# Split attention and a max-out MLP on one core: first loads in another order, score runs cut alike, the whole order planned anew

## The chip, the cores and the metric

The kernel runs on one core of a Trainium2 chip. The metric is the device time of one execution in microseconds, as the median of several runs. PE is the matmul engine (PEld its weight loads), DVE, ACT and POOL (GpSimd) are the vector, scalar and general engines, SP (SyncE) issues most DMAs. SBUF is the on-chip memory, PSUM holds matmul results in eight banks.

## What is computed

Attention over 4 batches, 8 heads, 768 positions, head size 64. Three "retrieval" heads see all earlier positions; the five others see 4 sink positions and a window of 64. Its output, as 3072 rows of 512, goes through an MLP that takes the larger of two products.

```python
scores = scale * np.matmul(q, k.transpose(0, 1, 3, 2))
mask = np.where(retr, causal, causal & (is_sink | in_win))   # by head
a = softmax(np.where(mask, scores, -1e9))
x = np.matmul(a, v)          # transposed to [B * S, H * D] = [3072, 512]
g = np.maximum(x @ w1, x @ w2)
out = g @ w_out
```

The kernel uses max(h1, h2) = relu(h1 - h2) + h2: with w12 = w1 - w2 and w2o = w2 @ w_out it computes out = relu(x @ w12) @ w_out + x @ w2o.

## The kernel before

**Tiling.** Each batch is cut in two halves of 384 query positions, (b, hf). Heads go in pairs; `SLOTS` says which pairs hold full (F) and which windowed (S) heads. In the text A = (0,0), B = (0,1), C = (1,0).

**Stages of a half.** q, k (768 KB each) and v (three pieces of 256 KB) are loaded into one of three slots of `ld`. They are cast to bf16 (`cast_qk`, `cast_v` into `vb`), q and k are turned by PE (L756) and copied from PSUM (`unturn`, into `qk`); for windowed heads the sink blocks are joined to window blocks (`mix_k`, `mix_v`, tiles `kx`, `vx`). Scores are matmuls in groups of two PSUM banks (L945; for A a bias at L919), exponentials run on ACT (L964), masks on DVE (L983), attention times v is L1008, normalising L1025 and L1035. The result x is turned, by PE for batch 0 (L1128) and by DMA for the others, into `xt`. Then come eight up blocks of 4 matmuls (L1219), a relu each (L1243 or L1245, on ACT or DVE), and three output blocks of 12 down matmuls (L1269), copied out by ACT or DVE (`ot`) and stored by SP (L1288).

**Weights.** w1 and w2 are loaded as f32 in halves of 1 MB (L637): w2 into the third slot of `ld`, w1 into the slot of A, so that w1 has to wait until A's q, k and v have been cast. w_out goes in four loads through GpSimd's queue, which cast to bf16 (L651). `prep_weights` casts w2, turns it (L1180), multiplies it with w_out in 32 matmuls (L1198) and subtracts w1 - w2 in four quarters on DVE (L1164). The first up block needs the first of these quarters.

**The order.** Nothing is scheduled by hand. Every piece of work is an `Op` with costs per engine, dependencies and a rank. `Order.run` plays them through a model of the engines, the DMA queues and the PSUM banks, and emits each instruction when the model starts it. So constants such as `RANK`, `FRONT`, `MARGIN`, `RATE`, `DMA_LATE` and `RING` (how much may be outstanding on a queue) decide the order of each engine's instructions, and nothing else. The engines then run these orders with real waits. Where the model leaves PE idle in the first 38 us, it puts in matmuls on a tile `warmer` (L503). `LOADS` names the order in which the first loads are asked for: A and B are q and k of a half, Av and Bv its v, wo0 to wo3, w10 to w21 the weights.

A load of w_out waits for an earlier load by way of a one-element copy on GpSimd (`landed`, L650); `PACE` says how far behind in the flow.

Of the kernel before, what the change touches and what calls it, by code (L numbers as in the profile page):

```python
# [114 lines left out]
class Op:  # L115
# [4 lines left out]
        "claims", "frees", "margin", "tag", "port", "bias", "share", "parts", "grain",  # L120
    )

    def __init__(self, costs, emit, deps=(), lat=0.13, data=None, rank=0.0, claims=(), frees=(),
                 margin=0.0, tag=None, port=(), bias=None, share=1.0, parts=1024, grain=18.0):
        self.costs, self.emit, self.lat, self.data, self.rank = costs, emit, lat, data, rank
        self.deps = [o for o in deps if o is not None]
        self.claims, self.frees, self.margin, self.tag = claims, frees, margin, tag
        self.port, self.bias, self.share, self.parts = port, bias or {}, share, parts
        self.grain = grain
        self.end, self.ready, self.users = None, 0.0, []  # L130


class Order:
# [6 lines left out]
    def __init__(self, banks, dummy, dummies_until):  # L140
        self.ops, self.lists, self.n, self.shift, self.stuck = [], {}, 0, 0.0, False
        self.banks, self.freed = [None] * banks, [0.0] * banks
        self.at, self.dummy, self.dummies_until = {}, dummy, dummies_until
# [36 lines left out]
    def release(self, key, t):  # L180
        key, part = key if isinstance(key[-1], list) else (key, None)
        for e in self.at[key] if part is None else [self.at[key][part[0]]]:
            assert self.banks[e] == key
            self.banks[e], self.freed[e] = None, t
# [12 lines left out]
    def run(self, names, allowed):  # L197
        free = dict.fromkeys(("PE", "ACT", "DVE", "POOL", "SP"), 0.0)
        free["SP"], free["PE"] = 0.75, PE_BEGINS
# [26 lines left out]
        def begin(o, e, t, extra=0.0):  # L226
            cost = o.costs[e] + extra
            if e in o.port:
                wait = max(0.0, port[0] - t)
                cost += wait  # L230
                port[0] = t + cost
            free[e] = t + cost
            if e == "PE":
                done_pe.append((t, t + cost, o.share))
            o.emit(e)
            trace.append((t, e, cost, o))
            push(t + cost, None)
            if o.data is None:
                push(t + cost + o.lat, o)
            else:  # L240
                asked[e] += o.parts
                push(t + (DMA_FIRST if t < 1.0 else DMA_LATE[e]), (e, o))

# [34 lines left out]
        for t in (0.0, free["SP"], free["PE"]):  # L278
            push(t, None)
# [107 lines left out]
    'cast': 8.0, 'vcast': 10.45, 'unturn': 6.55, 'mix_k': -4.7, 'mix_v': -16.7, 'exp': 3.7,  # L387
    'mask': -7.6, 'norm': -7.5, 'take_x': -1.15, 'turn': 0.05, 'w2b': 5.75, 'sub': -6.2, 'w2t':
    -4.8, 'wob': -3.6, 'w2o': -3.6, 'relu': 3.45, 'load': 6.6, 'out': -5.4, 'h2': 7.9, 'table':
    -3.65, 'vload': -0.55,  # L390
# [14 lines left out]
LOADS = ('A', 'wo0', 'B', 'w20', 'w10', 'Av', 'wo1', 'wo2', 'w11', 'wo3', 'w21', 'Bv')  # L405
# [11 lines left out]
DMA_LATE = {'SP': 2.7, 'POOL': 3.2, 'ACT': 2.2}  # L417
RING = {'SP': 4224, 'POOL': 6200, 'ACT': 4224}
SPLIT = ((0, 0), (0, 1))
K_BY_ACT = False  # L420
# [7 lines left out]
    'first': 0.26, 'long': 0.32, 'v': 0.235, 'w': 0.355, 'w half': 0.39, 'wo': 0.37, 'cast':  # L428
    0.22,
}  # L430
SPARE = {}
STEP = 3.5
FF_STEP = -2.8
# [9 lines left out]
MARGIN = {'W': 1.2, 'S': 0.3, 'F': 0.3, 'TQ': 1.2}  # L443
X_MARGIN = 0.8
FRONT = (
    {'mix_k': -14.4, 'mask': -3.2, 'unturn': 13.5, 'exp': 11.7, 'vcast': 31.8, 'cast': -27.9,
    'norm': -5.0}, {'vcast': 9.0, 'unturn': -0.2, 'exp': 16.7, 'mask': 0.7, 'norm': -5.5,
    'mix_k': 13.8, 'cast': -1.4},
)
FRONT_STEP = (22.5, 5.2)  # L450
UNTURN_BIAS = ({'ACT': 1.0}, {})
SHARED = 0.89
UP_PARTS = 2


def tile_three_full_heads(
# [36 lines left out]
    landed = keep.tile([1, 1], F32, name="landed")  # L493
# [13 lines left out]
    eng = {"ACT": nc.scalar, "DVE": nc.vector, "POOL": nc.gpsimd}  # L507
    T = {}
# [18 lines left out]
    def dma(mb, emit, deps=(), rate=0.31, rank=0.0, old=None, parts=1024, grain=18.0):  # L527
        asked.append(rank)
        o = op({"SP": 0.5}, emit, deps, data=mb / rate, rank=rank + 1e-4 * len(asked), parts=parts, grain=grain)
        if old is not None:  # L530
            later.append((o, old))
        return o
# [4 lines left out]
    def slot():  # L537

        s = PLACES[number[0]]
        number[0] += 1  # L540
        old, freed[s] = freed.get(s, []), []
        return s, old, freed[s]

    def load_half(b, hf, kinds=(0, 1, 2)):
# [4 lines left out]
        def whole(t, src):  # L549
            def emit(_):  # L550
                nc.sync.dma_start(  # L551
                    out=lds[:, s, t],
                    in_=src[b, :, rows, :].rearrange("h (p n) d -> p h (n d)", p=128),
                )
            mb = 1.572 if early_k and (b, hf) == (0, 0) else 0.786
            loads[b, hf, t].append(dma(mb, emit, old=old, rate=RATE["first"] if t == 0 and (b, hf) != (0, 0) else RATE["long"], grain=36.0))

        def piece(t, src, i):
            def emit(_):
                r0 = HALF * hf + 128 * i  # L560
                nc.sync.dma_start(
                    out=lds[:, s, t, :, i * D:i * D + D],
                    in_=src[b, :, r0:r0 + 128, :].rearrange("h p d -> p h d"),
                )
            loads[b, hf, t].append(dma(0.262, emit, old=old, rate=RATE["v"]))
# [26 lines left out]
    def load_pair(b, p):  # L592
# [32 lines left out]
        tenants[b].append(un)  # L625
        return un, [got[2, 0], got[2, 1]]

    def load_up(name, src, c):

        if name not in T:  # L630
            s, staged_old[name], tenants[name] = slot()
            T[name] = lds[:, s].rearrange("p t h c -> p (t h c)")[:, 0:KC * d_ff] \
                .rearrange("p (c f) -> p c f", f=d_ff)
        n = d_ff // UP_PARTS

        def emit(_):
            nc.sync.dma_start(  # L637
                out=T[name][:, :, c * n:c * n + n],
                in_=src.rearrange("(c p) f -> p c f", p=128)[:, :, c * n:c * n + n],
            )  # L640
        return dma(
            2.097 / UP_PARTS, emit, old=staged_old[name], rate=RATE["w"] if UP_PARTS == 4 else RATE["w half"],
            parts=512, grain=180.0 / UP_PARTS,
        )

    def load_down(c, behind):

        def emit(_):
            for o in behind:
                nc.gpsimd.tensor_copy(out=landed, in_=place_of[o])  # L650
            nc.gpsimd.dma_start(  # L651
                out=wob[:, 2 * c:2 * c + 2],
                in_=wo.rearrange("(c p) f -> p c f", p=128)[:, 2 * c:2 * c + 2],
            )
# [7 lines left out]
    for what in LOADS:  # L662
        kind, c = what[:2], int(what[2:]) if what[:1] == "w" else 0
        if what[0] in "ABCD":
# [4 lines left out]
            for n, o in enumerate(loads[(*of, kinds[-1])]):  # L669
                last = (n if kinds[-1] == 2 or of not in LONG else NT - 1) * D  # L670
                place_of[o] = lds[0:1, slot_of[of], kinds[-1], 0, last:last + 1]
        elif kind == "wo":
            wo_in[c] = load_down(c, flow[-1 - PACE:len(flow) - PACE])
        else:
# [3 lines left out]
            place_of[got[c]] = T[kind + "f"][0:1, 0, c * d_ff // UP_PARTS:c * d_ff // UP_PARTS + 1]  # L678
# [47 lines left out]
    def cast_qk(n, hf, hh, lo=0, hi=2):  # L726
        b, p = first_half(n)

        def emit(e):
            src = lds[:, slot_of[b, hf], lo:hi, bass.ds(heads[2 * p + hh], 1), :]  # L730
# [30 lines left out]
    def unturn(n, hf, lo=0, hi=2):  # L761
        def emit(e):
            src = bank(("pt", n, hf, lo), BF16)[:, 0:(hi - lo) * HALF].rearrange("f (t c) -> f t c", t=hi - lo)
# [61 lines left out]
    def prepare(b, hf, p):  # L825
# [7 lines left out]
        else:  # L833
# [4 lines left out]
            for hh in range(2):  # L838
                for lo, hi in ((0, 1), (1, 2)) if (b, hf) in SPLIT else ((0, 2),):
                    cs.append(op(  # L840
# [4 lines left out]
                    ))  # L845
            casts[n, hf] = cs
# [11 lines left out]
            tenants[b, hf] += cs + (vs if b not in V_BY_DMA else [])  # L858
# [8 lines left out]
            else:  # L867
                last_turn[n, hf], turned[n, hf] = [], []
                for lo, hi in ((0, 1), (1, 2)) if (b, hf) in SPLIT else ((0, 2),):
                    key, m = ("pt", n, hf, lo), hi - lo  # L870
                    tq = pe(
                        "TK" if lo else "TQ", mm(*[128] * (m * NT)), turn(n, hf, lo, hi),
                        cs[lo::2] if m == 1 else cs, claims=[(key, 1)],
# [5 lines left out]
                        frees=[key], tag=f"unturn{b}.{hf}.{p}", rank=rank_of("unturn", b, hf, p),  # L879
# [27 lines left out]
    def scores(b, hf, t):  # L907
        banks_, _, _ = group_of(b, hf)[t]

        def emit(_):  # L910
# [10 lines left out]
            for bk, blocks in enumerate(banks_):  # L921
# [9 lines left out]
                runs.append(mine)  # L931
            for step in range(max(len(r) for r in runs)):
# [113 lines left out]
    def attend(b, hf):  # L1046
        group = group_of(b, hf)
        exps, done = {}, {}
        for t in range(len(group)):
# [20 lines left out]
            for bk in range(2):  # L1070
# [4 lines left out]
                if len(at_users) > NAT:  # L1075
                    later.append((e, at_users[-1 - NAT]))
# [80 lines left out]
    def prep_weights():  # L1157
# [31 lines left out]
        tenants["w2f"] += w2b_ops + sub_ops  # L1189
        tenants["w1f"] += sub_ops  # L1190
# [164 lines left out]
    for e, old in later:  # L1355
        e.deps.extend(old)
# [323 lines left out]
```

## Time and profile before

| | us |
|---|---|
| median of 3 runs | 182.96 (182.65 to 184.0) |
| profiled run, device time | 182.93 |
| its span in the profile | 181.3 |
| PE busy | 174.2 (96%) |
| ACT busy | 132.1 (73%) |
| DVE busy | 101.7 (56%) |
| mean granted PE clock | 0.988 of full |

The span runs from the first to the last instruction of the profile; 1.63 us of the device time lie around it. In the profile a row of a group gives line, engine, operation, tiles, shapes and count, then busy us and the mean ns of one, then the idle time before them and what ended it. `ps` are the PSUM banks.

### The profile page before, as it was taken

The page shows a single profiled execution, that of the slowest core. Times are in us where ns is not written, and L with a number is a line of the kernel's source. Part 1 is how long each engine was busy: PE and PEld are TensorE (multiplying, and loading weights), DVE is VectorE, ACT ScalarE, POOL GpSimd, SP SyncE. Part 2 cuts the span into 40 slices and gives each one's busy share as a digit, 9 for nine tenths or more (in the row PEclk, how much of TensorE's full clock was granted, in tenths as well). Part 3 has the DMA queues.
Part 4 walks back from the last instruction along what each step waited for, and adds up shares of the span by engine and source line. Part 5 has one row for each costly group of instructions (what it writes and reads, how often), then busy time and mean ns, then how long its engine had stood idle before and what let it go on. Part 6 is the DMA issues. An engine that isn't in the chain of part 4 may idle for free.

```text
span 181.3 us, 4989 instructions
## 1 busy us (share of the span) xinstructions
PE 174.2 (96%) x1838; PEld 108.7 (60%) x1838; DVE 101.7 (56%) x303; ACT 132.1 (73%) x294; POOL 40.1 (22%) x80
## 2 busy tenths in 40 slices
PE   7996999999999999999989999999999999999992
PEld 7965776457657656556645775465565545545561
DVE  5685687699979998377875687247455300000000
ACT  3466846999799999999999998379694614624521
POOL 6503500200413583778930000000000000000000
PEclk9997899999999999999999999999999999999998
DMA  4999999999999999999999999620312412012013
GB/s 119 334 291 338 227 263 256 384 241 276 255 303 317 299 252 193 281 189 214 133 150 150 157 250 115 170 91 0 90 58 96 110 58 108 17 61 116 0 58 125
DMA packets 72529, 32.37 MB, mean 179 GB/s; under 512 B 53938, under 2 KB 67506, under 8 KB 72498
## 3 DMA queue, kind: packets, MB, share of 16 engines
q1 hardware_dynamic: 52448, 28.45, 62.4%
q0 software_dynamic: 19904, 3.41, 25.7%
q8 instruction: 16, 0.26, 0.6%
q14 instruction: 15, 0.12, 0.2%
q10 hardware_dynamic: 146, 0.13, 0.2%
HBM read 25.17 MB, written 6.29 MB: 174 GB/s over the span
## 4 chain that ended last, share of the span: by engine, by line
PE 70%; DMA 13%; DVE 7%; ACT 4%; issue 2%; SPq 2%; DVEq 0%; POOL 0%; ACTq 0%; POOLq 0%
PE ps L1269 31%; PE ps L1219 20%; DMA ld<-in_k_dram 7%; PE ps L945 7%; PE ps L1008 6%; DMA ld<-in_moe_w_dram 6%; PE ps L756 2%; ACT at L964 2%; DVE x L1035 2%; SPq L551 2%; PE ps L503 1%; ACT vb L512 1%; DVE at L983 1%; DVE qb L514 1%; PE ps L1198 1%
## 5 line engine op out<-in xcount | busy, mean ns | idle before, releaser
L964 ACT ACTIVATE at<-ps 128x512 bf16<-128x512 f32 (+2 forms) x134 | 66.1, 590 | 5.2 <-PE ps L945 4.5
L1269 PE MATMUL ps<-wob,g 128*128 128x512 bf16 (+1 forms) x200 | 47.6, 371 | 0.0
L1219 PE MATMUL ps<-xt,w 128*128 128x384 bf16 x256 | 45.8, 326 | 0.3 <-DVE w L1164 0.3
L983 DVE TENSOR_TENSOR at<-at,tab 128x1024 bf16<-128x1024 bf16 (+5 forms) x49 | 24.5, 514 | 14.9 <-ACT at L964 14.5
L1219 PEld LDWEIGHTS <-w 128*128 128x128 bf16 x256 | 23.5, 98 | 15.5 <-DVE w L1164 0.4
L1243 ACT ACTIVATE g<-ps 128x384 bf16<-128x384 f32 x56 | 27.8, 507 | 4.4 <-PE ps L1219 4.2
L512 ACT COPY ot<-ps 128x512 f32<-128x512 f32 (+1 forms) x21 | 12.0, 573 | 25.9 <-PE ps L1269 25.9
L1269 PEld LDWEIGHTS <-g 128*128 128x128 bf16 x200 | 18.2, 98 | 17.9 <-issue 0.2
L1269 PE MATMUL ps<-w2o,xt 128*128 128x512 bf16 (+1 forms) x100 | 24.8, 370 | 0.3 <-ACT ot L512 0.2
L1008 PEld LDWEIGHTS <-at 128*128 128x128 bf16 x477 | 20.0, 97 | 7.6 <-issue 0.2
L1035 DVE TENSOR_TENSOR x<-ps,rez 128x192 f32 x64 | 22.8, 356 | 1.8
L1008 PE MATMUL ps<-vb,at 128*128 128x65 bf16 x387 | 21.4, 193 | 0.0
L945 PE MATMUL ps<-qk 64*128 64x128 bf16 (+1 forms) x322 | 19.8, 230 | 0.1
L945 PEld LDWEIGHTS <-qk 64*128 64x128 bf16 x322 | 12.0, 94 | 9.1 <-issue 6.8
L503 PE MATMUL ps<-warmer 128*128 128x128 bf16 x149 | 14.3, 258 | 1.4 <-POOL warmer L1613 1.2
L1269 PEld LDWEIGHTS <-xt 128*128 128x128 bf16 x100 | 9.2, 98 | 9.0 <-issue 0.5
L756 PE MATMUL ps<-tab,qb 128*128 128x128 bf16 x144 | 12.6, 227 | 1.7 <-POOL qb L514 1.2
L514 POOL CAST vb<-ld 128x192 bf16 x21 | 8.1, 424 | 26.2 <-DMA ld<-in_v_dram 26.2
L503 PEld LDWEIGHTS <-warmer 128*128 128x128 bf16 x149 | 12.2, 119 | 1.5 <-POOL warmer L1613 1.2
L514 DVE COPY qk<-ps 128x384 bf16<-128x384 bf16 (+1 forms) x17 | 10.2, 642 | 3.9 <-PE ps L756 3.9
L512 ACT CAST qb<-ld 128x192 bf16 (+1 forms) x26 | 9.5, 425 | 3.8 <-DMA ld<-in_k_dram 2.0
L756 PEld LDWEIGHTS <-qb 128*128 128x128 bf16 x144 | 9.6, 101 | 3.8 <-POOL qb L514 1.4
(70 smaller groups left out, 159.6 us busy)
## 6 DMA issues: line engine op xcount, KB each, us to landing
out_dram<-ot SPq DMA_DIRECT2D x23, 256.0 KB, 2.1
ld<-in_q_dram SPq DMA_DIRECT2D x6, 768.0 KB, 7.5
ld<-in_k_dram SPq DMA_DIRECT2D x6, 768.0 KB, 7.9
ld<-in_v_dram SPq DMA_DIRECT2D x18, 256.0 KB, 6.9
ld<-in_moe_w_dram SPq DMA_DIRECT2D x4, 1024.0 KB, 11.7
wob<-in_moe_w_out_dram POOLq DMA_DIRECT2D x4, 256.0 KB, 7.8
ld<-in_q_dram POOLq DMA_DIRECT2D x8, 96.0 KB, 9.0
ld<-in_k_dram POOLq DMA_DIRECT2D x8, 96.0 KB, 9.7
```

The costliest lines, as they stand in the source:

```text
L503: nc.tensor.matmul(banks[e][:, 0:128], lhsT=warm, rhs=warm, start=True, stop=True)
L512: nc.scalar.copy(out=out, in_=in_)
L514: eng[e].tensor_copy(out=out, in_=in_)
L756: nc.tensor.transpose(to[:, i], qbs[:, T["qb", n, hf] % NQB, t, i].rearrange("p h d -> p (h d)"), ident)
L945: nc.tensor.matmul(to.rearrange("p (i c) -> p i c", c=128), lhsT=lhsT, rhs=q_of(n, i, m)[rows], start=bk not in under, stop=True, skip_gro ...
L964: nc.scalar.activation(out=at[:, bk, 0:w], in_=bank(("ps", b, hf, t), part=bk)[:, 0:w], func=ACT.Exp, scale=scale,)
L983: eng[e].tensor_tensor(out=at, in0=at, in1=tbl, op=ALU.mult)
L1008: nc.tensor.matmul(po[:, hh, i - NT * hf, :], lhsT=ats[:, T["at", b, hf, t] % NAT, bk, e * 128:(e + 1) * 128], rhs=rhs, start=first, stop= ...
L1035: nc.vector.tensor_tensor(out=xs[:, (2 * b + hf) % NX, :, bass.ds(heads[2 * p + hh], 1), :], in0=po[:, hh, :, 0:D].unsqueeze(2), in1=z[:, ...
L1219: nc.tensor.matmul(bank(key)[:, 0:HALF], lhsT=w[:, kc, fc * 128:(fc + 1) * 128], rhs=xts[:, (2 * b + hf) % NXT, :, kc, :], start=(kc == 0) ...
L1243: nc.scalar.activation(out=g, in_=ph, func=ACT.Relu)
L1269: nc.tensor.matmul(bank(key)[:, cols], lhsT=lhsT, rhs=(w2o if kind == "x" else wob)[:, c, cols], start=(e == 0), stop=(e == len(steps) - 1),)
```

## The change

Three things are changed, and much is added that stays switched off.

The first loads are asked for in another order, with w_out behind A's v:

```diff
-LOADS = ('A', 'wo0', 'B', 'w20', 'w10', 'Av', 'wo1', 'wo2', 'w11', 'wo3', 'w21', 'Bv')
+LOADS = ('A', 'B', 'Av', 'wo0', 'wo1', 'w20', 'wo2', 'wo3', 'w10', 'w21', 'w11', 'Bv')
```

Where the two banks of a group of scores hold runs of unequal number (adjacent blocks of one key block are merged into one wide matmul), all runs are cut into blocks of 128 columns:

```diff
+            if len(runs[0]) != len(runs[1]):
+                runs = [
+                    [[bk, e + j, (*blk[:-1], blk[-1] + j), 1, hh, p] for bk, e, blk, m, hh, p in mine for j in range(m)]
+                    for mine in runs
+                ]
```

The model has new limits and the constants of the order are new (ranks, steps and fronts not shown; all of them are changed):

```diff
-        free["SP"], free["PE"] = 0.75, PE_BEGINS
+        free["SP"], free["PE"], free["POOL"] = 0.75, PE_BEGINS, MASKS_MADE - 0.45
...
-                push(t + (DMA_FIRST if t < 1.0 else DMA_LATE[e]), (e, o))
+                o.late = DMA_FIRST if t < 1.0 else max(RING_LATE, DMA_LATE[e] - max(0.0, t - max(o.ready, idle[e])))
+                push(t + o.late, (e, o))
...
-DMA_LATE = {'SP': 2.7, 'POOL': 3.2, 'ACT': 2.2}
-RING = {'SP': 4224, 'POOL': 6200, 'ACT': 4224}
+DMA_LATE = {'SP': 2.7, 'POOL': 4.7, 'ACT': 2.2}
+RING_LATE = 1.0
+RING = {'SP': 3300, 'POOL': 6200, 'ACT': 4224}
...
-            parts=512, grain=180.0 / UP_PARTS,
+            parts=1536 // UP_PARTS, grain=180.0 / UP_PARTS, rank=-9.0 if by_act else 0.0,
...
-MARGIN = {'W': 1.2, 'S': 0.3, 'F': 0.3, 'TQ': 1.2}
-X_MARGIN = 0.8
+MARGIN = {'W': 0.5, 'S': 2.0, 'F': 2.0, 'TQ': 2.0}
+X_MARGIN = 0.4
```

`MARGIN` is how long an operation must have been ready, in the model, before PE takes it while other work is there; S are scores, W attention times v, F the MLP, TQ the turning of q and k.

What a slot of `ld` waits for is now kept by kind: q, k and v of a half each wait for the readers of that kind alone in the model; a weight still waits for all three.

```diff
-            loads[b, hf, t].append(dma(0.262, emit, old=old, rate=RATE["v"]))
+            loads[b, hf, t].append(dma(
+                0.262, emit, old=old[t:t + 1], rate=RATE["v"], rank=0.0 if by == "SP" else RANK["vload"], by=by,
+            ))
```

`SIX`, `BY_ACT` and `V_QUEUES`, which would lay halves out in 64 rows or send loads over other queues, are added empty, and `landed` has 128 rows in place of one for their sake.

More of the change, by code (lines that the diff above doesn't have):

```diff
@@ L845, in prepare @@
                     ))
+                    leaves((b, hf), range(lo, hi), [cast])
             casts[n, hf] = cs
@@ L857, in prepare @@
                 ))
-            tenants[b, hf] += cs + (vs if b not in V_BY_DMA else [])
+            leaves((b, hf), (2,), vs if b not in V_BY_DMA else ())
             key = ("pt", n, hf)
```

142 lines of the change are left out of this document (99 added, 43 removed).

## The prediction

> **What bounds the kernel now.** I read the page first, then the engines by stretches, then the chain of waits in order of time, then the issues of SyncE and GpSimd with the transfer rate under them. From the page (busy us, share of the span, instructions; then one group with busy us and mean ns):
>
> ```profile
> span 181.3 us, 4989 instructions
> PE 174.2 (96%) x1838; PEld 108.7 (60%) x1838; DVE 101.7 (56%) x303; ACT 132.1 (73%) x294; POOL 40.1 (22%) x80
> L503 PE MATMUL ps<-warmer 128*128 128x128 bf16 x149 | 14.3, 258 | 1.4 <-POOL warmer L1613 1.2
> ```
>
> PE is 96% busy, but 14.3 us of that is fill-in matmuls on `warmer` that compute nothing. The next rows say where PE is full of real work; columns are the stretch, its length, then busy us of PE, PEld, DVE, ACT and POOL, the granted clock, DMA share and GB/s.
>
> ```profile
> 38.10:140.00 101.90, 101.25 (x1186) 62.43 (x1187) 72.94 (x208) 90.84 (x204) 29.32 (x47) 1.00 1.11 183
> 140.00:178.00 38.00, 37.97 (x210) 20.23 (x208) 2.55 (x11) 16.35 (x32) 0.00 (x0) 1.00 0.21 75
> ```
>
> From 38.10 to 178 PE is idle 0.68 us in all, at full clock. So time can be won only before 38.10. The chain of waits (start, us, what) tells what holds that point:
>
> ```profile
> 3.84 11.87 DMA ld<-in_k_dram
> ...
> 22.87 1.31 PE ps L1198 x6
> ...
> 25.36 11.44 DMA ld<-in_moe_w_dram
> ...
> 36.82 1.24 DVE w L1164
> 38.10 2.77 PE ps L1219 x16
> 40.87 0.78 PE ps L945 x24
> 41.65 2.71 PE ps L1219 x16
> 44.36 0.88 PE ps L1008 x29
> ...
> 170.17 7.81 PE ps L1269 x48
> 178.01 0.37 ACT ot L512
> ```
>
> The first half of w1 lands at 25.36 + 11.44 = 36.80; the subtraction w1 - w2 takes 1.24; at 38.10 the first up-projection starts; 139.91 us later the last down-projection ends, at 178.01. That is the sum of the kernel: *landing of w1, plus 1.30, plus 139.9, plus the tail*. The issues of SyncE, in order, with how long each took to issue:
>
> ```profile
> 6.08 2.33 SPq L637 DMA_DIRECT2D ld<-in_moe_w_dram  x1
> 8.46 9.66 SPq L561 DMA_DIRECT2D ld<-in_v_dram  x3
> 18.16 0.93 SPq L637 DMA_DIRECT2D ld<-in_moe_w_dram  x1
> 19.14 5.96 SPq L561 DMA_DIRECT2D ld<-in_v_dram  x3
> 25.36 4.90 SPq L637 DMA_DIRECT2D ld<-in_moe_w_dram  x2
> ```
>
> Ahead of w1 stand q and k of A = (0,0) and B = (0,1), both halves of w2, all three v pieces of A and all three of B. And the rate beneath:
>
> ```profile
> 3.00:11.00 8.00, 7.97 (x110) 7.26 (x109) 5.95 (x22) 2.93 (x11) 4.09 (x10) 1.00 1.08 328
> 18.00:21.00 3.00, 3.00 (x30) 1.97 (x29) 2.52 (x9) 2.21 (x5) 0.68 (x2) 0.72 0.87 162
> 19.00:20.00 1.00, 1.00 (x9) 0.60 (x6) 1.00 (x2) 0.98 (x2) 0.00 (x0) 0.65 0.96 212
> 26.00:29.00 3.00, 2.98 (x41) 2.33 (x39) 2.93 (x10) 1.24 (x2) 0.00 (x0) 1.00 1.22 198
> 31.00:34.00 3.00, 3.00 (x22) 1.28 (x20) 1.47 (x3) 2.88 (x7) 0.00 (x0) 1.00 1.07 386
> ```
>
> The DMA engines are at a share near 1 all the way; only around 18 to 21 does it dip (0.87, 162 GB/s). So w1 lands when the bytes queued ahead of it are through, and its wait for A's v casts, which end just before 25.36, is covered by that queue.
>
> **The change, part by part.**
>
> *Loads.* In the built order SyncE issues q, k of A and B, the three v pieces of A, w2 (two halves), *one* v piece of B, w1 (two halves), then the other two v pieces of B. So 2 x 256 KB = 0.524 MB no longer precede w1. At 212 GB/s, the row in which only v pieces were in flight, that is 2.5 us; at 386 GB/s it would be 1.4, at 198 GB/s (beside w_out) 2.6. I take 2.5, since v pieces are what goes. w1's first half then lands at 34.3. Its issue must wait for A's v casts, which now wait only for A's v, issued before w2; in the trace of before they stood here:
>
> ```profile
> 22.46 1.12 ACT L512 CAST vb<-ld 128x192 bf16 x4
> 23.16 1.12 DVE L514 CAST vb<-ld 128x192 bf16 x4
> 34.18 0.92 POOL L514 CAST vb<-ld 128x192 bf16 x3 [11.25 <-DMA ld<-in_v_dram]
> 35.01 1.58 DVE L514 COPY vx<-vb 64x204 bf16<-64x204 bf16 x6
> ```
>
> Seven of the eight are now on ACT, 7 x 0.28 = 2.0 us; they are over by about 20, and w2 and the v piece cover the queue past that. If that cover were gone (w1 issued later than 34.3 - 11.4 = 22.9), each us late would be a us lost.
>
> *w_out.* One of its four loads went at 6.17, beside q and k, the rest at 20.53 to 22.21; now all four go behind A's second and third v piece (two each).
>
> ```profile
> 6.17 0.83 POOL L651 DMA_DIRECT2D wob<-in_moe_w_out_dram  x1
> 20.53 0.72 POOL L651 DMA_DIRECT2D wob<-in_moe_w_out_dram  x1
> 22.21 0.72 POOL L651 DMA_DIRECT2D wob<-in_moe_w_out_dram  x1
> DMA to landing us min/median/max: 7.4/8.3/9.4
> ```
>
> (The last row: the three late loads, landing 27.9 to 31.6, 1.85 apart.) The bytes ahead of w1 are the same, so the shift costs nothing in the sum: between one w_out load's length sooner and as much later, 1.85 us either way, 0 taken. The small copies that make GpSimd wait go from three to four, 0.2 us on an engine that has nothing else due there but v casts of B, which wait for their data. B's k no longer shares the line with w_out and lands before the 15.7 of the chain; that only feeds scores, which do not end last.
>
> *What else must be ready for the first up-projection.* On PE, which runs in order, there now stand before it the whole of w2's product with w_out (32 matmuls, as before the change at this point) and 26 more score matmuls, while 30 attention-times-v matmuls move behind it. At 0.78/24 = 0.0325 and 0.88/29 = 0.0303 us that is 0.85 more before and 0.91 more behind: nothing in sum, as long as PE gets there in time. Its last links: the fourth w_out load, then 6 matmuls (1.31), 24 scores (0.78), 8 matmuls (1.75), together 3.84. If A's second and third v piece land by 17.5 and the last w_out is issued by 19.2 and needs the longest landing, 9.4, this gives 28.6 + 3.84 = 32.4, 3.2 us before w1 allows it. ACT is closer: from 11 to the first up-projection it has 28 exponentials instead of 25, and was busy
>
> ```profile
> 20.00:25.00 5.00, 5.00 (x83) 3.55 (x83) 3.00 (x11) 3.05 (x8) 2.61 (x6) 1.00 1.05 290
> 25.00:30.00 5.00, 4.98 (x83) 3.70 (x80) 4.21 (x14) 2.21 (x3) 0.00 (x0) 1.00 1.23 204
> L964 ACT ACTIVATE at<-ps 128x512 bf16<-128x512 f32 (+2 forms) x134 | 66.1, 590 | 5.2 <-PE ps L945 4.5
> ```
>
> 4.74 of these 10 us idle; three more at 0.59 are 1.8, the 2.5 us lost at the end 2.5: 4.3 of 4.74. It fits, barely. First up-projection: 34.3 + 1.30 = 35.6.
>
> *Behind it.* The 32 up matmuls now stand in one run, and each quarter needs its subtraction. w1's second half came 2.7 us after the first:
>
> ```profile
> DMA to landing us min/median/max: 11.4/11.7/12.0
> ```
>
> (two issues, 25.36 and 27.52, so 36.8 and 39.5). So it lands at 37.0, the last two subtractions end at 38.3 and 39.5, and the run ends near 40.9, about 0.1 later than unhindered. Then come 59 attention-times-v matmuls that need B's v. Its last two pieces follow w1, 2.5 us after 37.0, at 39.5; from its landing to the last of `vx` it took 36.6 - 34.0 = 2.6, so they are complete at 42.1, 1.2 after the run. Part of the 59 need only early pieces of this: 0.6 taken, between 0 and 1.2. C's q and k go right behind v, 2 x 0.786 MB at 328 GB/s = 4.8, so 44.3, before the turn of C, which stands 24 + 8 + 16 attention and down matmuls further.
>
> *Score runs.* In four groups one matmul of 384 columns becomes three of 128: 8 more, at most 8 x 0.0325 = 0.26 dearer; a gain is as possible, since they now alternate with three of the other head. 0 taken.
>
> *The later order* is new, but PE has the same work and the same 22 runs of scores behind the first up-projection, and the tail from the last attention on is the same. At most the 0.68 us idle can be won; ACT, full there, could cost as much. 0 taken.
>
> Sum: 2.5 - 0.1 - 0.6 = 1.8 us. The profiled run took 182.93 (span 181.30 and 1.63 around it), the median is 182.96: 182.93 - 1.8 = **181.1**.
>
> **Rivals.**
> 1. *More is won.* The dip at 18 to 21 goes too, because w2's second half is no longer issued behind a blocked SyncE (9.66 us for three v pieces). For it: 162 GB/s against 212 is 0.7 us, against 386 it is 1.7; middle 1.2, so 179.9. Against it: ACT and PE, which leave little beyond 35.6.
> 2. *The lag of w_out.* The chain has B's k landing at 15.71, though A and B are 3.15 MB, 9.6 us at 328 GB/s from about 3.0, plus 1.35 for one w_out load at 386: 14.0. Beside w_out a transfer is late by some 1 us more than its bytes, and that one lag was made up in the dip, ahead of w1. With all four loads in the run-up to w1 and no dip, w1 carries it: 181.1 + 1.0 = 182.1. The Trainium skill, DMA: Bandwidth & Descriptors, section Latency and other measured facts, says that two of the sixteen DMA engines are usually slower, with GpSimd's descriptor rings as a guess at the cause; by that rule a transfer lands with the slowest engine and this case is the right one. The rows here show the late landing, not the engine.
> 3. *Slower: the w_out loads become the bound.* They now run beside w2's long rows instead of v's. If each takes twice its 1.85, the last lands at 16.5 + 8.3 + 3 x 3.7 = 35.9, and PE reaches the up-projection at 39.7, 4.1 later than forecast: 185.2. It decides from 35.6 - 3.84 = 31.8 on. Against it: while they ran, they held their pace against v (198 GB/s counted), and 2.6 us of slack.
> 4. *The order does not do what it plans*: the same point, held by ACT, at 38.1, lies within rival 2's range.
>
> **How the numbers follow.** Forecast 0.40 (180.4 to 181.8), rival 1 0.26 (178.9 to 180.4), rival 2 with 4 0.22 (181.8 to 183.0), rival 3 0.12 (183.0 to 186). A measurement of this kernel can tell about 1%, 1.83 us, so faster means below 181.1: rival 1 and half of the forecast less a little, 0.47. Slower, above 184.8, is most of rival 3: 0.10. The rest, 0.43, is within 1%. The range for 8 in 10 leaves out rival 3 and the far end of rival 1: 179.0 to 183.3.
>
> **What would show it.** Right: w1's first half lands near 34.3, the first up matmul starts near 35.6, and 140 to 141 us lie from there to the last down matmul. Wrong: w1 lands above 35.5 although nothing but one v piece of B is ahead of it (rival 2); PE fills in or waits at the 32 product matmuls for `wob` (rival 3); ACT without a gap from 20 to 36 and w1 landed before it is subtracted; or over 1 us idle at the 59 matmuls behind the up run.

## The result, and the profile after

The changed kernel took 183.70 us (median of 21 runs, 182.72 to 185.86), the kernel before 182.92 beside it. The ratio is 1.0056, with a 95% interval of 1.003 to 1.0081: half a per cent slower, where 181.1 was forecast, and above the range of 179.0 to 183.3. In some kernels a few executions are over 1.5% longer than the fastest one; the ratios leave these out, the medians do not. The profiled run took 183.75, its span 182.1.

The page of the changed kernel, first lines (busy us, share of the span, instructions):

```profile
span 182.1 us, 5021 instructions
PE 173.6 (95%) x1847; PEld 107.4 (59%) x1847; DVE 100.9 (55%) x303; ACT 133.9 (74%) x295; POOL 41.0 (23%) x80
```

The chain of waits of the changed kernel, in order of time (start, us, what), from the first of the four w_out loads to the first up-projection. Lines have moved: L1272 is the product with w_out, L1202 the turn of x, L1254 that of w2, L1019 the scores, L1293 the up-projection.

```profile
16.82 8.71 DMA wob<-in_moe_w_out_dram
...
25.56 0.59 PE ps L1272 x2
26.16 0.67 PE ps L1202 x12
26.82 0.89 PE ps L1254 x16
27.72 1.29 PE ps L1272 x6
29.01 0.71 PE ps L1019 x9
29.72 3.56 PE ps L1272 x16
33.28 0.78 PE ps L1019 x24
34.06 1.83 PE ps L1272 x8
```

and its end:

```profile
170.83 7.81 PE ps L1343 x48
...
178.67 0.37 ACT ot L523
```

The first up matmul starts at 35.73 instead of 38.10: 2.37 us won, as forecast. The last down-projection ends at 178.64 instead of 177.98: 0.66 later. So what lies between has grown from 139.9 to 142.9, and 3.0 us were lost there. The engines by stretches show where (columns as in the prediction: length, busy us of PE, PEld, DVE, ACT, POOL, clock, DMA share, GB/s):

```profile
35.73:140.00 104.27, 101.44 (x1195) 61.93 (x1194) 72.55 (x211) 90.82 (x202) 31.17 (x50) 1.00 1.13 186
140.00:178.67 38.67, 38.63 (x218) 20.65 (x214) 3.15 (x13) 16.80 (x34) 0.00 (x0) 1.00 0.21 73
35.73:55.00 19.27, 19.27 (x217) 12.10 (x216) 16.06 (x45) 15.87 (x37) 3.68 (x7) 1.00 1.02 267
55.00:60.00 5.00, 4.16 (x52) 2.75 (x51) 4.54 (x13) 4.76 (x12) 3.52 (x10) 1.00 1.05 285
90.00:100.00 10.00, 8.18 (x94) 4.16 (x91) 4.35 (x12) 9.31 (x23) 7.21 (x10) 1.00 2.07 170
```

From the first up-projection on PE idles 2.83 + 0.04 = 2.87 us; before it was 0.68. That is 2.19 of the 3.0. It sits in two holes, 0.84 us in 55 to 60 and 1.82 in 90 to 100. In the other 0.8, PE is busy. Adding up each matmul's time to the start of the next, in the two traces: the 30 attention-times-v matmuls that now stand behind the first up-projection make these 0.77 us longer; the scores there take 0.22 less (26 matmuls moved ahead, 8 added by the cut); and about 0.3 is in up, down and turning matmuls whose number has not changed.

The same stretches of the kernel before have hardly a hole: 5.00 us busy in 55 to 60, and 0.59 us idle in 90 to 100:

```profile
90.00:100.00 10.00, 9.41 (x101) 4.98 (x99) 6.14 (x17) 9.81 (x25) 2.24 (x3) 1.00 2.08 147
```

What PE waits for in the second hole can be followed back on ScalarE. Its instructions in order in the changed kernel (start, us, operation, and in brackets how long it stood idle and for what):

```profile
85.45 0.87 ACT L1317 ACTIVATE g<-ps 128x384 bf16<-128x384 f32 x2
87.89 0.35 ACT L523 CAST vb<-ld 128x192 bf16 x1 [1.57 <-DMA ld<-in_v_dram]
88.15 1.33 ACT L523 CAST qb<-ld 128x384 bf16 x3
```

ScalarE takes its list in order here: it waits 1.57 us for the last v piece of (2,1), and the casts of q and k and the copies of the turn, for which scores wait, stand behind it. k, which landed at 82.01, waits with them. Now SyncE's issues, in the changed kernel and then in the kernel before (start, us that the issue took; L1221 and L1147 are the transpose of x, L1362 and L1288 the stores):

```profile
66.27 4.79 SPq L1221 DMA_TRANSPOSE xt<-x  x1
71.16 0.53 SPq L596 DMA_DIRECT2D ld<-in_v_dram  x1
71.79 0.63 SPq L1362 DMA_DIRECT2D out_dram<-ot  x1
72.47 0.42 SPq L583 DMA_DIRECT2D ld<-in_k_dram  x1
72.95 2.48 SPq L596 DMA_DIRECT2D ld<-in_v_dram  x1
75.52 3.16 SPq L1362 DMA_DIRECT2D out_dram<-ot  x1
78.73 0.44 SPq L596 DMA_DIRECT2D ld<-in_v_dram  x1
```

```profile
65.14 3.02 SPq L1147 DMA_TRANSPOSE xt<-x  x1
68.27 0.51 SPq L561 DMA_DIRECT2D ld<-in_v_dram  x1
68.84 1.27 SPq L551 DMA_DIRECT2D ld<-in_k_dram  x1
70.16 2.13 SPq L561 DMA_DIRECT2D ld<-in_v_dram  x1
73.46 0.36 SPq L1288 DMA_DIRECT2D out_dram<-ot  x1
73.86 1.34 SPq L561 DMA_DIRECT2D ld<-in_v_dram  x1
```

Before, three of the four loads of (2,1) went out in one run and one store stood ahead of the last. Now two stores stand between them, and the second took 3.16 us to issue where the one before took 0.36. The last v piece goes out 4.87 us later (78.73 against 73.86), though PE is ahead, and it lands at 78.73 + 9.14 = 87.87 instead of 82.88. Not all of that is the stores: v piece 0, ahead of both, is already 2.89 us later (71.16 against 68.27), since the transpose of x goes out 1.13 us later and takes 1.77 longer to issue. No run takes that part by itself. The first hole looks alike: k of (1,1) stands behind a store that was not there before, goes out at 47.95 instead of 45.88 and lands at 55.34 instead of 53.29, while PE is some 2.5 us ahead and needs it sooner.

### The profile page after: what moved, and what is told of

Its sections match the earlier page's. It is cut to its first block, busy times and chain, and to the rows that moved or that the text cites. A ratio compares the mean times of both kernels' runs of the same rounds, so it can differ in the third digit from the quotient of the medians.

```text
span 182.1 us, 5021 instructions
## 1 busy us (share of the span) xinstructions
PE 173.6 (95%) x1847; PEld 107.4 (59%) x1847; DVE 100.9 (55%) x303; ACT 133.9 (74%) x295; POOL 41.0 (23%) x80
## 4 chain that ended last, share of the span: by engine, by line
PE 60%; DMA 18%; SPq 8%; ACT 7%; issue 3%; DVE 1%; ACTq 0%; DVEq 0%; POOL 0%
PE ps L1343 25%; PE ps L1293 18%; DMA ld<-in_v_dram 10%; PE ps L1019 6%; PE ps L1082 5%; DMA wob<-in_moe_w_out_dram 5%; SPq L596 5%; DMA ld<-in_k_dram 4%; PE ps L1272 4%; SPq L583 3%; ACT at L1038 2%; PE ps L805 1%; ACT vb L523 1%; ACT qk L523 1%; ACT ot L523 1%
## 5 line engine op out<-in xcount | busy, mean ns | idle before, releaser
L1038 ACT ACTIVATE at<-ps 128x512 bf16<-128x512 f32 (+2 forms) x134 | 63.8, 589 | 2.9 <-PE ps L1019 2.8
L1343 PE MATMUL ps<-wob,g 128*128 128x512 bf16 (+1 forms) x200 | 46.7, 371 | 0.0
L1293 PE MATMUL ps<-xt,w 128*128 128x384 bf16 x256 | 45.6, 326 | 0.2 <-DVE x L1109 0.2
L1293 PEld LDWEIGHTS <-w 128*128 128x128 bf16 x256 | 23.7, 98 | 15.6 <-issue 0.6
L523 ACT COPY ot<-ps 128x512 f32<-128x512 f32 (+1 forms) x23 | 13.4, 582 | 23.1 <-PE ps L1343 22.9
L1317 ACT ACTIVATE g<-ps 128x384 bf16<-128x384 f32 x52 | 25.6, 500 | 6.2 <-PE ps L1293 5.9
L1082 PEld LDWEIGHTS <-at 128*128 128x128 bf16 x477 | 19.1, 97 | 6.7 <-issue 0.7
L1019 PE MATMUL ps<-qk 64*128 64x128 bf16 (+1 forms) x330 | 20.2, 228 | 2.1 <-DVE g L1319 0.8
L1019 PEld LDWEIGHTS <-qk 64*128 64x128 bf16 x330 | 12.4, 94 | 12.7 <-issue 9.7
L525 POOL CAST vb<-ld 128x192 bf16 x21 | 8.8, 455 | 26.4 <-DMA ld<-in_v_dram 25.4
L523 ACT COPY qk<-ps 128x768 bf16<-128x768 bf16 (+1 forms) x17 | 12.5, 771 | 2.9 <-PE ps L805 2.3
L513 PEld LDWEIGHTS <-warmer 128*128 128x128 bf16 x150 | 11.4, 116 | 1.4 <-POOL warmer L1687 1.2
L525 DVE CAST qb<-ld 128x384 bf16 (+1 forms) x30 | 9.5, 371 | 4.6 <-DMA ld<-in_k_dram 2.5
L805 PE MATMUL ps<-tab,qb 128*128 128x128 bf16 x144 | 11.2, 219 | 0.8 <-DVE qk L525 0.6
## 6 DMA issues: line engine op xcount, KB each, us to landing
ld<-in_moe_w_dram SPq DMA_DIRECT2D x4, 1024.0 KB, 13.4
```

What stands on the lines that cost most here:

```text
L513: nc.tensor.matmul(banks[e][:, 0:128], lhsT=warm, rhs=warm, start=True, stop=True)
L523: nc.scalar.copy(out=out, in_=in_)
L525: eng[e].tensor_copy(out=out, in_=in_)
L805: nc.tensor.transpose(to[:, i], qbs[:, T["qb", n, hf] % NQB, t, i].rearrange("p h d -> p (h d)"), ident)
L1019: nc.tensor.matmul(to.rearrange("p (i c) -> p i c", c=128), lhsT=lhsT, rhs=q_of(n, i, m)[rows], start=bk not in under, stop=True, skip_gro ...
L1038: nc.scalar.activation(out=at[:, bk, 0:w], in_=bank(("ps", b, hf, t), part=bk)[:, 0:w], func=ACT.Exp, scale=scale,)
```

## The experiments

Four theories were on the table. **1b**: the order of SyncE's issues makes the holes. **1a**: the transfers are full from 70 to 90 us and GpSimd's early loads of batch 3 take the share that (2,1) needs. (These loads are not new: four of them went out at 72.70 to 75.14 before, and go out at 71.87 to 74.30 now.) **2**: ScalarE, busy over 95% there, sets the pace whatever lands. **3**: the cut of the score runs costs.

The edits leave the plan as it is and move finished entries of it before they are emitted, so that every other instruction keeps its place. `MOVES` holds pairs, what is moved and ahead of what, all on SyncE; (k, 2, 1) is the load of k for (2,1), (v, 2, 1, i) its v pieces, xt the transpose of x, out the stores by number.

```diff
+def moved(put):
+    for what, ahead_of in MOVES:
+        places = {o.tag: n for n, (e, o, _) in enumerate(put) if o is not None and e == "SP"}
+        put.insert(places[ahead_of], put.pop(places[what]))
+    return put
```

Each ratio is to the kernel before on the same chip; the changed kernel's is 1.0056. Where a kernel is said to be faster or slower than the changed kernel, that is the difference of the two ratios, of 182.9 us.

**The loads of (2,1) back in the old order.**

```diff
+MOVES = [(('k', 2, 1), ('out', 3, 0)), (('v', 2, 1, 1), ('out', 3, 0)), (('v', 2, 1, 2), ('out', 3, 0))]
```

> In the changed kernel, k and v pieces 1 and 2 of (2,1) go out on SyncE ahead of the store that stands between them and v piece 0; the transpose of x stays ahead of all four, and GpSimd's loads stay. This is the order that the kernel before had there: transpose, v 0, k, v 1, v 2, then stores. Theory 1b (SyncE's order, here the three stores between the loads): v piece 2 is issued near 74.5 instead of 78.73, lands near 83 to 84.5 instead of 87.87, and the run is 0.7 to 1.5 us faster than the changed kernel. If instead the sum of what the transfers carry between 70 and 90 us sets the landing (theory 1a), the piece goes out earlier and still lands after 86, and the gain is under 0.5 us.

Measured: 181.99 us, ratio 0.9962 (0.9934 to 0.9991), about 1.7 us faster than the changed kernel (1.0 to 2.4 by the two intervals) and 0.7 under the kernel before. SyncE and ScalarE of this kernel:

```profile
72.13 4.91 SPq L610 DMA_DIRECT2D ld<-in_v_dram  x2
77.14 4.05 SPq L1376 DMA_DIRECT2D out_dram<-ot  x3
```

```profile
86.23 0.35 ACT L537 CAST vb<-ld 128x192 bf16 x1 [0.44 <-DMA ld<-in_v_dram]
```

ScalarE's wait is 0.44 us instead of 1.57, and PE is busy 4.39 and 4.60 us in 90 to 95 and 95 to 100, where the changed kernel had

```profile
90.00:95.00 5.00, 4.33 (x50) 2.17 (x47) 1.82 (x6) 4.35 (x11) 4.99 (x8) 1.00 2.06 166
95.00:100.00 5.00, 3.85 (x48) 1.99 (x45) 2.54 (x6) 4.96 (x14) 2.22 (x3) 1.00 2.09 173
```

(Of the three stores in that stretch two stood between the loads; the third already followed them.) The gain is a little above what theory 1b expected; the landing is what theory 1a expected, after 86: the piece, the second of the two in the row at 72.13, went out 3.8 us earlier (74.93) and landed only 1.7 earlier, at 86.13 rather than 83 to 84.5. So the order counts, and part of what it wins at the issue is lost again in the transfers. Theory 2 is out as the reason of the loss: ScalarE is busy 4.96 of 5 us in 95 to 100 here as in the changed kernel, and PE has 4.60 instead of 3.85.

**GpSimd's loads of batch 3 later.** Six of them go behind its second cast of (2,1).

```diff
+    loads = [n for n in pool if put[n][1].tag == "load3.1"][:4] + [n for n in pool if put[n][1].tag == "load3.2"][:2]
+    casts = [n for n in pool if put[n][1].tag.startswith("cast2.1.")]
+    behind = put[casts[1]]
...
+    put[at + 1:at + 1] = group
```

> In the changed kernel, four of GpSimd's loads of batch 3 (the q and k of its second pair of heads, issued 71.87 to 74.30 us and landed 80.0 to 86.7) and the next two go out behind the casts of (2,1) that GpSimd does at 82 to 84 us. SyncE's order stays. Theory 1a (the loads of (2,1) come late because the transfers are full between 70 and 90 us, and GpSimd's loads share them): k of (2,1) lands 1 to 3 us before 82.01 and v piece 2 some 2 to 3 us before 87.87, and the run is 0.5 to 1.5 us faster than the changed kernel, unless the transpose of that pair of batch 3, at 92.5 us, now comes late. Theory 1b (only SyncE's order counts): both land within 0.5 us of where they did, no gain. ScalarE's pace (theory 2): landings earlier, no gain.

Measured: 181.79 us, ratio 0.9961 (0.9934 to 0.9987), some 1.7 us faster than the changed kernel and a little above theory 1a's 0.5 to 1.5. The issues between 70 and 90 us with their median time to landing, in the changed kernel and in this one:

```profile
ld<-in_v_dram SPq DMA_DIRECT2D x3, 256.0 KB, 8.7
ld<-in_k_dram SPq DMA_DIRECT2D x1, 768.0 KB, 9.5
```

```profile
ld<-in_v_dram SPq DMA_DIRECT2D x3, 256.0 KB, 7.3
ld<-in_k_dram SPq DMA_DIRECT2D x1, 768.0 KB, 7.5
```

k, issued at the same time (72.50 against 72.47), lands 2.0 us earlier. ScalarE no longer waits for the v piece at all, and PE's stretches are 4.66 and 4.60:

```profile
90.00:95.00 5.00, 4.66 (x45) 2.15 (x44) 3.30 (x10) 4.70 (x10) 5.00 (x7) 1.00 2.16 187
95.00:100.00 5.00, 4.60 (x47) 2.60 (x46) 2.79 (x9) 4.96 (x13) 0.91 (x2) 1.00 1.80 164
```

So SyncE's order is not the only lever: the same hole shrinks at least as much when the stores stay and the other queue's traffic goes. It is a lever and not what changed, since the kernel before had these loads at the same time. The Trainium skill, DMA: Bandwidth & Descriptors, section Queues, rings and completion order, says that each DMA engine takes turns between the queues that have work for it, packet by packet. The landings here agree with that: with the 96 KB loads of GpSimd's queue out of the way, k needed 7.5 us to land instead of 9.5. In the changed kernel they went out from 71.87 on, although the transpose that needs them went out only at 92.53.

**Everything of (2,1) ahead of the transpose of x.**

```diff
+MOVES = [(('k', 2, 1), ('xt', 1, 0)), (('v', 2, 1, 0), ('xt', 1, 0)), (('v', 2, 1, 1), ('xt', 1, 0)), (('v', 2, 1, 2), ('xt', 1, 0))]
```

> All four loads of (2,1) that still stand there, k and the three v pieces, go out on SyncE ahead of the transpose of x for (1,0). Theory 1b (SyncE's order alone): v piece 2 lands before 82 us, the hole at 90 to 100 us closes, 1.5 us or more faster than the changed kernel. Against it: the transpose of x goes out near 73 us instead of 66.27 and lands near 82 instead of 75.22; if the up-projection of (1,0) is then what TensorE lacks, a hole of some 3 us appears at 77 to 83 us and nothing is gained. That would make the stretch a matter of how much the transfers move, not of their order.

Measured: 192.47 us, ratio 1.0548 (1.0501 to 1.0596). The price named against it came, far larger than named. The chain and the stretches of this kernel:

```profile
74.38 12.31 DMA xt<-x
...
86.74 1.46 PE ps L1307 x4
```

```profile
75.00:80.00 5.00, 2.70 (x30) 1.27 (x28) 3.13 (x4) 4.96 (x13) 5.00 (x9) 1.00 2.07 172
80.00:85.00 5.00, 0.00 (x0) 0.00 (x0) 0.00 (x0) 0.24 (x1) 3.44 (x7) 0.69 1.98 105
85.00:90.00 5.00, 3.26 (x21) 1.91 (x22) 0.82 (x2) 0.04 (x1) 2.66 (x4) 0.50 1.67 247
90.00:95.00 5.00, 5.00 (x40) 2.79 (x38) 3.70 (x11) 3.68 (x9) 3.08 (x4) 0.78 2.12 156
```

The transpose goes out at 74.38 and lands at 86.69; PE's up-projection waits for it. PE has nothing at all from 77.70 to 86.74, and then runs at a granted clock of 0.50 up to about 92. So the transpose has less slack here than the loads of (2,1), and by the two experiments above the stores and batch 3 have more.

**k and two v pieces, with k ahead of the transpose.**

```diff
+MOVES = [(('k', 2, 1), ('xt', 1, 0)), (('v', 2, 1, 1), ('out', 3, 0)), (('v', 2, 1, 2), ('out', 3, 0))]
```

> Three SyncE issues are moved in the changed kernel: the load of k for (2,1) goes out ahead of the transpose of x for (1,0), and v pieces 1 and 2 of (2,1) ahead of the store that they stand behind. Nothing else changes. Theory 1: k of (2,1) is issued near 67 us rather than 72.47 and v piece 2 near 73 rather than 78.73, landing near 76 and 82 as in the kernel before (77.23 and 82.88); TensorE's 4.33 and 3.85 us in the stretches 90 to 95 and 95 to 100 rise to 4.5 and 4.9 as before, and the run is 1.0 to 1.8 us faster than the changed kernel, that is 182 to 182.7 and level with the kernel before or below it. Theory 2 (ScalarE's pace): under 0.5 us. A cost on the other side: the transpose of x goes out up to 3 us later and may hold up the up-projection of its batch; then the same or slower.

Measured: 182.99 us, ratio 1.0014 (0.9984 to 1.0044): some 0.8 us gained, below the 1.0 to 1.8 of theory 1; the interval overlaps with that of the changed kernel. The transpose now landed at 78.4 instead of 75.2, and PE was busy 4.13 us of 5 in 75 to 80. With k left behind the transpose (the first experiment), twice as much is won.

**The same with GpSimd's later loads.**

```diff
+MOVES = [(('k', 2, 1), ('xt', 1, 0)), (('v', 2, 1, 1), ('out', 3, 0)), (('v', 2, 1, 2), ('out', 3, 0))]
...
+    put[at + 1:at + 1] = group
```

> The moves of k and two v pieces of (2,1) that brought 0.7 us, together with GpSimd's later loads of batch 3. If both act on the same scarce transfers, v piece 2 of (2,1) lands near 83 us as in the kernel before, TensorE's 4.17 and 4.52 us in 90 to 100 us rise to 4.5 and 4.9, and the run is 0.5 to 1 us faster than with the moves alone: 182.0 to 182.5.

Measured: 182.11 us, ratio 0.9966 (0.994 to 0.9991), as GpSimd's move alone. The transpose lands at 78.45 here too; that it takes back what the earlier loads bring fits this, but is not shown apart.

**The first hole: k of (1,1) ahead of the first store.**

```diff
+MOVES = [(('k', 1, 1), ('out', 0, 0))]
```

> One SyncE issue is moved in the changed kernel: the load of k for D = (1,1) goes out ahead of the first store instead of behind it and D's first v piece (issued at 47.95 us, landed at 55.34). All other instructions of all engines stay as they are. Theory 1 (the order of the loads in the middle makes the holes): the load is issued near 46.5 us and lands near 54, TensorE's 4.16 us of work in the stretch 55 to 60 us rises towards 4.8, and the run is 0.3 to 0.9 us faster than the changed kernel. Theory 2 (ScalarE, busy over 95% from 50 us on, sets the pace anyway): the hole shrinks but the end moves by less than 0.2 us, since the later hole at 90 to 100 us is set by loads that this edit does not touch.

Measured: 186.25 us, ratio 1.0192 (1.0144 to 1.0239), 2.5 us slower than the changed kernel, a miss. The first hole did close, 5.00 us busy in 55 to 60. But the v pieces of (1,1) came later, GpSimd's casts of them with them, and its loads of batch 3, which follow those casts, began at 62.07 instead of 60.40. The transpose of x and k of (2,1) landed 2.7 and 2.8 us later (77.95, and 73.84 + 11.00 = 84.84), and PE lost more at 80 to 90 than it had won, 2.74 us of it in one hole that ends at 86.56. Which of these steps starts the chain was not taken apart.

**k of (1,1) and the loads of (2,1) as above, k ahead of the transpose.**

```diff
+MOVES = [(('k', 2, 1), ('xt', 1, 0)), (('v', 2, 1, 1), ('out', 3, 0)), (('v', 2, 1, 2), ('out', 3, 0)), (('k', 1, 1), ('out', 0, 0))]
```

> Both of the moves above in one kernel. Theory 1: the gains add, 1.5 to 2.5 us faster than the changed kernel, 181.2 to 182.2, which is where the prediction stood (181.1) and under the kernel before. Theory 2: under 0.5 us, 183.2 or more. If the two holes are one chain, both together bring no more than the larger one alone.

Measured: 187.50 us, ratio 1.0239 (1.0189 to 1.0289). Nothing adds, and the 1.5 to 2.5 us forecast as gained are missed by far; the cost of moving k of (1,1) alone stays.

**The first hole with GpSimd's loads out of the way.** v piece 0 keeps its place ahead of k, both go ahead of the store, and GpSimd's six loads are later.

```diff
+MOVES = [(('v', 1, 1, 0), ('out', 0, 0)), (('k', 1, 1), ('out', 0, 0))]
...
+    put[at + 1:at + 1] = group
```

> GpSimd's move, and v piece 0 and k of D = (1,1) on SyncE ahead of the first store (the store goes behind both). With k alone moved the run lost some 2.5 us, k landing 1.5 us earlier and everything behind it on the queue 1 to 2 us later. If that loss came from the place of k in the queue (a large load next to be moved while v pieces and stores wait), it stays here in part: 182.5 to 184. If it came from GpSimd's loads colliding with later loads, it is gone, k lands near 54.4 and the hole at 55 to 60 us shrinks from 1.05 to under 0.5 us: 181.2 to 181.8.

Measured: 181.53 us, ratio 0.9927 (0.9907 to 0.9947), 0.6 us under GpSimd's move alone, though the intervals still touch. k landed at 53.07, sooner than when it alone was moved (46.28 + 7.57 = 53.85), and the first hole is gone:

```profile
55.00:60.00 5.00, 5.00 (x71) 3.67 (x70) 4.85 (x14) 5.00 (x13) 3.13 (x9) 1.00 0.97 268
```

**Stores behind (2,1), and GpSimd later.**

```diff
+MOVES = [(('k', 2, 1), ('out', 3, 0)), (('v', 2, 1, 1), ('out', 3, 0)), (('v', 2, 1, 2), ('out', 3, 0))]
...
+    put[at + 1:at + 1] = group
```

> The same order on SyncE together with GpSimd's six later loads of batch 3 (which alone brought 1.9 us). If the two act on one bound, the arrival of (2,1), and ScalarE's work of 4.9 us in each 5 us comes next, this is within 0.4 us of GpSimd's move alone: 181.4 to 182.2. If they add, 180.5 to 181.2.

Measured: 181.74 us, ratio 0.9946 (0.9925 to 0.9968). As the first case of the forecast has it, they act on one bound and hardly add.

**All three moves.**

```diff
+MOVES = [(('v', 1, 1, 0), ('out', 0, 0)), (('k', 1, 1), ('out', 0, 0)), (('k', 2, 1), ('out', 3, 0)), (('v', 2, 1, 1), ('out', 3, 0)), (('v', 2, 1, 2), ('out', 3, 0))]
...
+    put[at + 1:at + 1] = group
```

> All three moves together: GpSimd's six loads later, the loads of (2,1) ahead of the stores, v piece 0 and k of (1,1) ahead of the first store. If each removes its own hole: 180.5 to 181.5, which is the predicted 181.1 or below. If the place of k of (1,1) costs what it cost alone, above 182.5.

Measured: 181.46 us, ratio 0.9917 (0.9887 to 0.9946): faster than both kernels, by 0.8% than the one before and some 2.5 us than the changed one. The first hole is smaller but not gone, with PE busy 4.66 us in 55 to 60. Against the two moves of (1,1) and GpSimd (0.9927) no further gain can be told.

**The score runs not cut.** The four added lines are taken out; the plan is otherwise the same.

```diff
-            if len(runs[0]) != len(runs[1]):
-                runs = [
...
-                ]
```

> The changed kernel without the cut of the score runs into blocks of 128: the 384-column matmuls of the scores come back, and everything else stays, the order of the other work too. Theory 3 (the cut costs: more matmuls, and more time at issue): 0.5 us or more faster. The prediction's own value: within 0.3 us of the changed kernel, either way.

Measured: 184.03 us, ratio 1.003 (0.9996 to 1.0063). Against 1.0056 (1.003 to 1.0081) no difference can be told. The 0.5 us of theory 3 would be 0.0027 of the ratio, which these intervals do not rule out. The trace speaks against it: behind the first up-projection the scores take PE 13.96 us in this kernel's profiled run, added up as above, and 13.97 with the cut.

**The order of the first loads alone, in the kernel before.**

```diff
-LOADS = ('A', 'wo0', 'B', 'w20', 'w10', 'Av', 'wo1', 'wo2', 'w11', 'wo3', 'w21', 'Bv')
+LOADS = ('A', 'B', 'Av', 'wo0', 'wo1', 'w20', 'wo2', 'wo3', 'w10', 'w21', 'w11', 'Bv')
```

> The kernel before with nothing changed but the order of its first loads (B's q and k, A's v, then the weights, as in the changed kernel); the planner orders the rest by the old limits and ranks. The planner itself puts this 2.1 us above the kernel before. If the front's gain comes from the order of the first loads and the loss in the middle from the new limits and ranks, this is faster than the kernel before by up to 2 us at 56 us of the span, and 181 to 182 in all. If the new order of loads needs the new ranks and limits (the loads of (1,0) and (1,1) come as late as they do in the changed kernel whoever plans), it is 183.5 to 185.

Measured: 184.51 us, ratio 1.0086 (1.0046 to 1.0127). With the old limits and ranks the planner put all of B's v ahead of w1, the first up-projection came at 39.39, and nothing was won in front. It was not w1 that held it, which landed at 35.18: the chain begins at the first w_out load, as in the changed kernel, and follows PE. The hole in the middle came all the same. SyncE, from the transpose of x on:

```profile
64.62 7.02 SPq L1147 DMA_TRANSPOSE xt<-x  x1
71.75 0.52 SPq L561 DMA_DIRECT2D ld<-in_v_dram  x1
72.32 0.85 SPq L551 DMA_DIRECT2D ld<-in_k_dram  x1
73.22 4.70 SPq L561 DMA_DIRECT2D ld<-in_v_dram  x1
78.03 2.46 SPq L1288 DMA_DIRECT2D out_dram<-ot  x1
80.53 0.43 SPq L561 DMA_DIRECT2D ld<-in_v_dram  x1
```

The last piece lands at 80.53 + 9.30 = 89.83, and the chain runs over it. But the order is that of the kernel before, with one store. What differs is how long the same issues took: 7.02, 4.70 and 2.46 us for transpose, v piece 1 and store, against 3.02, 2.13 and 0.36. So a second store among the loads is not needed for the late landing, and a plan made anew can fall into it with the old limits too. Why the issues took longer is open.

How far each kernel is ahead of the kernel before, in us, worked out from the matmuls in the traces: each counted by its columns, summed over time, without the fill-in, and the time compared at which the same sum is reached. The traces of the last three rows hold 2.4% fewer columns; the sums are scaled to one total, so a few tenths are uncertain. A column does not always take the same time (0.29 ns in the scores of the kernel before, 0.52 in attention times v), so an entry also moves with the order of the work.

```
at us                       40     55     60     90     95    100    140
changed kernel            +2.4   +2.6   +1.8   +1.2   +0.4   -0.8   -0.7
k of (1,1) ahead          +3.0   +3.1   +3.0   -1.3   -1.1   -1.5   -2.2
GpSimd's loads later      +2.9   +3.0   +2.0   +1.9   +1.8   +1.3   +1.3
stores behind (2,1)       +2.9   +3.0   +2.1   +2.1   +1.7   +1.3   +1.2
all three moves           +2.8   +3.0   +2.4   +2.4   +2.0   +1.4   +1.4
```

Half of the lead won in front is still there at 90 us. The changed kernel loses 0.8 of it at 55 to 60 and 2.0 at 90 to 100; the last three kernels lose 0.6 to 1.0 in each. With k of (1,1) moved alone, 4.3 us are lost between 60 and 90.

## Why the prediction was wrong, by its steps

**w1 lands at 34.3 for its 2.5 us less of v.** Right in its reason and too cautious: 33.4 (issued at 19.96, landed 13.4 later). The dip at 18 to 21 us went too, which is rival 1's condition: 386 GB/s there, where it had been 162.

**First up-projection at 35.6.** Right in size, 35.73, by luck: the cause is another. The first subtraction ran from 33.93 and was over at 35.15, so w1 no longer held it. The chain above shows what did, PE's own list behind w_out: the first of the four w_out loads, which went out at 16.82 instead of 6.17, landed at 25.52, and from 25.56 on PE works without a gap and without fill-in to 35.89. The fourth load was just in time: it landed at 31.79, and PE came to its first matmul at 31.83. The prediction had it in at 28.6, by 9.4 us from issue to landing; it took 12.2, and with the 3.84 of the last links that gives 35.6, not the 32.4 worked out. So w_out became the next bound, on the edge that rival 3 names (31.8), but not by its mechanism: the four loads landed 1.7, 1.8 and 2.7 us apart, not 3.7, and the cost was 0.1 us of the 4.1 it was priced at.

**0.7 us lost to the last subtractions and to B's late v.** Did not come: 35.73 to 55 is 19.27 us of which PE is busy 19.27; w1's second half landed at 36.2, not 37.0, and B's last v piece at 37.8, not 39.5. The matmuls that change sides of the first up-projection were set to nothing in sum, 0.85 ahead against 0.91 behind. They measure 0.55: 0.77 more behind it and only 0.22 less.

**Score runs cut, 0.** Within what can be told, and by the trace 0.

**"The later order is new, but PE has the same work... At most the 0.68 us idle can be won; ACT, full there, could cost as much. 0 taken."** This step failed, by 2.19 us: PE idles 2.87 us behind the first up-projection instead of 0.68, and 142.9 us lie from there to the last down-projection, where the prediction's own sign of being right was 140 to 141. The idle time before bounds what an order can win; it says nothing of what another order can lose. The bound that was set on the loss, ScalarE, had no row behind it, and the queue that mattered, SyncE's past the loads of C, was not walked. What came in the step's place is late loads: v of (2,1) lands at 87.87 instead of 82.88, k of (1,1) at 55.34 instead of 53.29. The planned order showed a part of it: two stores among the loads of (2,1), k of (1,1) behind a store. With those stores behind the loads of (2,1) again, and nothing else changed, the kernel takes 182.0 instead of 183.7; with GpSimd's loads moved as well 181.7, and with the moves of (1,1) on top 181.5. The longer issues are another part, which the planned order does not show. An estimate: 182.93 less the 2.37 of the front, plus the 0.8 in which PE is busy, is 181.4, near the forecast, had the middle stayed as dense as before.

**The rivals.** None of the four had the mechanism; the middle of the kernel was in no one's condition. Rival 1's dip went, without its gain, since w1 was no longer the bound. The lag of w_out (rival 2) did not show, w1 landing before it was forecast; by the rows named there it would have been 15.7 less 14.0, 1.7 us and not some 1. ScalarE as the bound in front (rival 4) did not show either: between 29 and 34 us it waits for PE, 1.16 and 1.01 us at a time.

What stays open: why the same issues on SyncE take longer in one plan than in another; why moving k of (1,1) alone costs 2.5 us; and how much of the difference to the run with v piece 0 ahead of it comes from that piece and how much from GpSimd's loads.

## What to carry to other kernels

When a plan is made anew, walk each DMA queue through the whole kernel and note for each load what stands ahead of it: idle time in the profile before bounds what can be won, not what can be lost. In a stretch where the transfers are full, look first for traffic that has slack, stores and loads for a later batch, and put that behind the load whose landing ends a wait. The other loads with little slack, here the transpose, must keep their place: passing it by with all four loads cost 9.0 us (1.0548 less 1.0056, of 182.9) where passing the stores won 1.7. And measure each move: k of (1,1) moved ahead of one store cost 2.5.

## What the runs showed of the hardware

A store of the same 256 KB took 0.36 us to issue in one place and 3.16 in another (the rows at 73.46 before and 75.52 after), and the load behind it on SyncE's list went out only then. A transpose took 3.02, 4.79 and 7.02 us to issue in three kernels. So the time of an issue is part of the price of a transfer, and what stands next in the list pays it.

PE left idle from 77.70 to 86.74 us came back at a granted clock of 0.50 in the 5 us from 85 on and 0.78 in the 5 after that (the rows of the kernel with everything ahead of the transpose). The Trainium skill, TensorE: Matmul & The Clock Gate, Part 1: The HAM clock gate, gives half rate after an idle window of about 3.4 us; the 0.50 here agrees, granted from 82 on, some 4 us into the hole. So that hole of 9.04 us cost more than its length. The shorter ones did not: the clock stayed at 1.00 through 2.74 us without a matmul with k of (1,1) moved alone, and through 3.24 us (78.90 to 82.14) with the loads of (2,1) moved as well.
